# Recurrent attention with a squared-relu layer on one core: weight casts on GpSimd, separate q and k transpose banks, more dummies at the start, later planned load times

## The chip, the cores and the metric

The kernel runs on one core of a Trainium2 chip. Its engines are TensorE (PE in the profile, with PEld for its weight loads), VectorE (DVE), ScalarE (ACT) and GpSimd (POOL); SyncE (SP) issues every DMA. The metric is the device time of one execution in microseconds; the median of three runs before the change is 195.5 us (195.12 to 195.73). Each engine takes its own instructions in the order in which they were written, and waits for the others by semaphores.

## The reference, cut to what matters

Four batches of eight heads, 768 tokens, head size 48. A state of 48 x 48 per head decays by `alpha` and takes up k times v; q reads it. All heads of a token together are a row of `x` (3072 tokens x 384), and the second part multiplies `x` with `w_in` (384 x 2048), squares the relu, and multiplies with `w_out` (2048 x 384).

```python
for t in range(S):
    state = alpha[:, :, t, :, None] * state + np.einsum('bhd,bhe->bhde', k[:, :, t], v[:, :, t])
    y[:, :, t] = np.einsum('bhd,bhde->bhe', q[:, :, t], state)
x = np.ascontiguousarray(y.transpose(0, 2, 1, 3)).reshape(B * S, H * D)
h = x @ w_in
r = np.maximum(h, 0.0)
out = (r * r) @ w_out
```

## The kernel before

**Tiles.** The 3072 tokens are 24 chunks of 128. Inside a chunk the recurrence becomes matmuls: the logarithm of alpha (`e_ln`, L563 on ACT) is summed along the tokens by a triangular matmul (`e_p0`, the only one with `utri_b`), A and Ainv are the exponentials of the sum with both signs (L582, L586 on ACT), `qA_s` and `kI_s` are q times A and k times Ainv (L601, L604 on DVE), PE turns both (`e_p1q`, `e_p1k`, four transposes each), DVE copies the turned tiles out of PSUM (L558), scores go to `sc`, DVE masks them into `sm` (L642), and PE multiplies with v (`vb`, cast by POOL at L568) and with the state. The result is copied to bf16 (`xn`, ACT L556), turned and stored in `xT_big`. The first four chunks go as two **sets** of two chunks each (`add_set`, L340), with instructions at L352 (ln), L380 (A and Ainv), L384 (products, one of them on POOL), L415 and L417 (copies of turned tiles on ACT and DVE), L454 (masks) and L485 (state).

**The layer behind it.** M1 is `xT_big` times `w_in_b` into a PSUM bank (three banks take turns), then relu on ACT (L746), then the square on DVE (L754, one tile `r` as both of its inputs) into `gT`. M2 is `w_out_b` times `gT`, sixteen matmuls of 128x384 for a chunk, in four quarters; the result leaves by L786 on ACT and a DMA (L794, L796). Chunks are grouped: the first group has four chunks, then one, one, and two at a time. M1 and M2 of ready chunks are the work that fills PE between the steps of the recurrence.

**Weights.** `load_w` (L277) loads w_in in five pieces (two of 128x768 float32, three of 128x1536) and w_out in four of 128x1536 into a four-buffer stage, and casts each to bf16. A piece's load waits for the cast of the piece four before it. The engine of a cast is picked by the planner: eight on DVE (L300), one on ACT (L302).

**Loads of the chunks.** `add_load` (L317) issues four DMAs a chunk (at, qt, kt, vt: alpha, q, k, v; 192 KB each, L324), `add_load2` (L330) four of 384 KB a set (L337). There are buffers for six chunks.

**The planner.** Nothing above is written in its final order. Each step is an `Op` with an engine, a planned duration, the ops it needs and a priority, and `Plan.run` places all ops on planned time lines; the instructions are then written out by planned start. A load has a planned duration and `lat`, the planned time from its end on the queue to its landing: 2.0 us for sets and chunks below 4, 2.4 us from chunk 4 on. An ACT op that needs a load (`e_ln`) is placed at the planned landing, with priority over the relus. What stands behind it on ACT waits with it. The gate (`LEAD`, L835) keeps `e_p0` of a chunk from being planned too far ahead of M1 and M2.

**Banks and dummies.** `GLA_BANKS` are two PSUM banks for all small steps of the recurrence; a `Slots` object says when a bank is free again (the op in `gives`). In `add_turn` (L420) a set's chunk j takes one bank for its turned q and its turned k together, so q of both chunks is turned first, then k of both into the same two banks. Until the first M2, planned gaps of PE are filled with dummy matmuls of a zero tile `warm` (L850 to L863): seven of 128x512 at the start, then one of 128x256 for each 0.11 us of a planned gap.

Of the kernel before, what the change touches and what calls it, by code (L numbers as in the profile page):

```python
# [9 lines left out]
BF16 = mybir.dt.bfloat16  # L10
# [9 lines left out]
class Slots:  # L20
# [5 lines left out]
    def free_at(self):  # L26
        n = len(self.release) - self.bufs
        if n < 0:
            return 0.0
        op = self.release[n]  # L30
        return None if op.done is None else op.done


LAT = {"PE": 0.13, "ACT": 0.14, "DVE": 0.13, "POOL": 0.25}
# [20 lines left out]
def after(op, x=0.0):  # L55
    return (op, x)
# [83 lines left out]
def kernel(  # L140
# [10 lines left out]
    nc = tc.nc  # L151
    B, H, S, D = q.shape
    HD = H * D
    P = 128
    DP = 64
    NP = H // 2
# [32 lines left out]
    ident_bf = consts.tile([P, P], BF16)  # L189
# [4 lines left out]
        out=utri_f, in_=utri_f, compare_op=ALU.is_ge, fill=0.0,  # L194
# [46 lines left out]
    def pin(ins):  # L241
        tc.keep_in_program_order(ins)
# [4 lines left out]
    def tr(*a):  # L247
        pin(nc.tensor.transpose(*a))  # L248

    plan = Plan()  # L250
# [4 lines left out]
    GLA_BANKS = sl_bank[0:2]  # L255
# [13 lines left out]
    def add(eng, dur, emit, *deps, **kw):  # L269
        return plan.add(Op(eng, dur, emit, deps, **kw))  # L270
# [6 lines left out]
    def load_w(which):  # L277
        j = len(w_ready[which])
        lo, hi = W_CUT[which][j:j + 2]
        n = hi - lo  # L280
        box = {}

        def halves(t):
            return t.rearrange("p j (a f) -> p a j f", a=2) if which == "i" else t
        if which == "i":
            src, dst = w_in_r[:, :, lo * P:hi * P], w_in_b[:, :, lo * P:hi * P]
            shape = [P, KT, n * P]
        else:
            src, dst = w_out_r[:, lo:hi, :], w_out_b[:, lo:hi, :]
            shape = [P, n, d_model]  # L290

        def e_issue():
            box["w"] = stage.tile(shape, FP32, name=f"w{which}{n}", tag="stage")
            pin(nc.sync.dma_start(out=box["w"], in_=src))

        def e_cast():
            if op.eng == "POOL":
                pin(nc.gpsimd.tensor_copy(dst, box["w"]))
            elif op.eng == "DVE":
                pin(nc.vector.tensor_copy(halves(dst), halves(box["w"])))  # L300
            else:
                pin(nc.scalar.copy(dst, box["w"]))  # L302
        prev = w_cast[-SB] if len(w_cast) >= SB else None
        ld = add("DMA", WLD * n / 4 + 0.03, e_issue, prev, lat=2.0)
        op = add({"POOL": 0.1 + 0.75 * n, "DVE": 0.1 + 0.2 * n, "ACT": 0.1 + 0.32 * n}, 0, e_cast, ld, prio=-3.0)
        w_cast.append(op)
        w_ready[which].append(op)

# [8 lines left out]
    def add_load(s, nm):  # L317
        d = C[s]
        b, c = divmod(s, NCH)

        def ld():
            i = s % LB
            d[nm] = ld_s[nm][:, i * HD:(i + 1) * HD].rearrange("p (h d) -> p h d", h=H)
            pin(nc.sync.dma_start(out=d[nm], in_=SRC[nm][b, c]))  # L324
        prev = C[s - LB]["use_" + nm] if s >= LB else None
        d["ld_" + nm] = add("DMA", LD if s < 4 else LD1, ld, prev, lat=2.0 if s < 4 else 2.4, at=0.6)

    E = [dict() for _ in range(NSET)]

    def add_load2(u, nm):  # L330
        d = E[u]

        def ld():
            t = ld_s[nm][:, 2 * u * HD:(2 * u + 2) * HD]
            d[nm] = t.rearrange("p (h j d) -> p h j d", h=H, j=2)
            b, c = divmod(2 * u, NCH)
            pin(nc.sync.dma_start(out=t.rearrange("p (h e) -> p h e", h=H), in_=srcs2[nm][b, c // 2]))  # L337
        d["ld_" + nm] = add("DMA", LD2, ld, lat=2.0, at=0.6)

    def add_set(u):  # L340
        d = E[u]
# [15 lines left out]
            pin(nc.gpsimd.tensor_copy(d["vb"], d["vt"].rearrange("p h j d -> p j h d")))  # L357
        vb = add("POOL", 1.1, e_vb, d["ld_vt"], prio=-5.0)

        pm, A, Ai, exA, exI, mq, mk, cps = {}, {}, {}, {}, {}, {}, {}, {}  # L360

        def add_sum(j):
            def e_p0():
# [40 lines left out]
        def e_cp(op, j, lo):  # L404
            if "qT" not in d:
                d["qT"] = work.tile([P, NP, 2, 2, HP], BF16, name="qT2", bufs=2)
                d["kT"] = work.tile([P, 2, NP, P], BF16, name="kT2", bufs=2)
            if lo:
                cast2(op, d["kT"][:, j], d["pT"][j][:, NP:, :])
            else:  # L410
                cast2(op, d["qT"][:, :, :, j, :], d["pT"][j][:, 0:NP, :].rearrange("q p (c i) -> q p c i", c=2))

        def cast2(op, out_t, in_t):
            if op.eng == "ACT":
                pin(nc.scalar.copy(out_t, in_t))  # L415
            else:
                pin(nc.vector.tensor_copy(out_t, in_t))  # L417
        d["pT"] = {}

        def add_turn(j):  # L420
            def e_p1q():
                d["pT"][j] = psum(p1q, [P, 2 * NP, P], BF16)
                for p in range(NP):
                    tr(d["pT"][j][:, p, :], qA[:, j, 2 * p:2 * p + 2, :], ident_bf)

            def e_p1k():
                for p in range(NP):
# [283 lines left out]
    gT = {}  # L711
# [11 lines left out]
    def add_moe1(g, f0, before, lo=0, hi=None, per=1):  # L723
# [26 lines left out]
        def e_sq():  # L750
            if g not in gT:
                gT[g] = big.tile([P, FT, P * max(GN[g % NGT::NGT])], BF16, name=f"gT{g % NGT}", tag=f"gT{g % NGT}")
            r = box["r"][:, 0:w].rearrange("p (a n) -> p a n", a=per)
            pin(nc.vector.tensor_mul(gT[g][:, f0:f0 + per, lo * P:lo * P + n], r, r))  # L754
# [139 lines left out]
```

## Time and profile before

| | us |
|---|---|
| median of three runs | 195.5 (195.12 to 195.73) |
| the profiled execution | 196.74 |
| its span, first to last instruction | 195.0 |
| PE busy in the span | 184.0 (94%) |
| DVE, ACT, POOL busy | 131.7, 121.7, 15.8 |
| mean granted TensorE clock | 0.988 |

The profiled execution took 196.74 us, of which the instructions span 195.0. A row of the timeline is: start in us from the span's start, duration in us, engine and line, operation, output <- inputs, shape, count of merged instructions, and in brackets the idle time of that engine ahead of it with what ended it. A row of the windows is a stretch, its length, busy us of the engines with their instruction counts, the granted clock of TensorE, the busy share of the DMA engines and what they moved. A row of the waits is: who waited for whom, us in all, how often, the longest.

### The profile page before, as it was taken

How to read it: one execution, taken by the hardware profiler on the slowest of the kernel's cores; microseconds unless marked ns; L12 is line 12 of the kernel's file. 1: busy time of each engine (PE TensorE's matmuls, PEld its weight loads, DVE VectorE, ACT ScalarE, POOL GpSimd, SP SyncE). 2: the span in 40 equal slices, each digit the busy share in tenths (PEclk: the TensorE clock that was granted, in tenths of full speed). 3: DMA queues.
4: the chain of work that ended last, by engine and by line, in shares of the span. 5: the costliest groups of instructions: out<-in, count | busy, mean ns of one | idle time of the engine just before them, and what ended most of it. 6: DMA issues, size and time to landing. Idle time of an engine off the chain costs nothing.

```text
span 195.0 us, 5155 instructions
## 1 busy us (share of the span) xinstructions
PE 184.0 (94%) x2051; PEld 137.2 (70%) x2051; DVE 131.7 (68%) x288; ACT 121.7 (62%) x283; POOL 15.8 (8%) x35
## 2 busy tenths in 40 slices
PE   6888999999999969999999999999999999999991
PEld 2656788667887646867867867867868768768660
DVE  5479999957987835876767858858757857735100
ACT  3557689446977564946956956956955746628210
POOL 3104001011101111111110110110010000000000
PEclk9999999999999978999999999999999999999998
DMA  6999999999899899999999999470110110111121
GB/s 151 261 264 369 379 195 318 262 201 166 186 196 205 150 198 207 187 203 205 194 216 178 212 162 195 91 179 4 40 44 0 42 45 0 44 40 40 44 81 42
DMA packets 99176, 30.22 MB, mean 155 GB/s; under 512 B 92112, under 2 KB 98000, under 8 KB 99152
## 3 DMA queue, kind: packets, MB, share of 16 engines
q1 hardware_dynamic: 99152, 29.89, 72.3%
q8 instruction: 16, 0.26, 0.6%
q14 instruction: 8, 0.07, 0.1%
HBM read 25.17 MB, written 4.72 MB: 153 GB/s over the span
## 4 chain that ended last, share of the span: by engine, by line
PE 82%; DMA 6%; ACT 3%; DVE 3%; SPq 1%; issue 1%; POOL 0%; ACTq 0%; POOLq 0%; DVEq 0%
PE bank L245 70%; PE bank L248 7%; DMA at_s<-in_alpha_dram 4%; PE sc L245 3%; DMA vt_s<-in_v_dram 2%; PE st L245 2%; ACT r L746 1%; SPq L324 1%; DVE kI_s L384 1%; SPq L794 0%; DVE qA_s L384 0%; ACT L_s L352 0%; DVE sm L454 0%; DVE kT L417 0%; ACT qT L415 0%
## 5 line engine op out<-in xcount | busy, mean ns | idle before, releaser
L245 PE MATMUL bank<-xT_big,w_in_b 128*128 128x256 bf16 (+1 forms) x624 | 77.5, 264 | 2.2 <-ACT r L746 2.1
L245 PE MATMUL bank<-w_out_b,gT 128*128 128x384 bf16 x384 | 72.6, 330 | 0.0
L746 ACT ACTIVATE r<-bank 128x512 bf16<-128x512 f32 x96 | 56.5, 603 | 19.8 <-PE bank L245 17.4
L245 PEld LDWEIGHTS <-w_in_b 128*128 128x128 bf16 x624 | 53.1, 98 | 9.2 <-issue 2.5
L754 DVE TENSOR_TENSOR gT<-r 128x512 bf16<-128x512 bf16 x96 | 38.2, 420 | 16.8 <-ACT r L746 16.7
L245 PEld LDWEIGHTS <-gT 128*128 128x128 bf16 x384 | 35.6, 98 | 19.7 <-issue 1.0
L642 DVE TENSOR_TENSOR sm<-sc,utri_b 128x512 bf16<-128x512 f32 x40 | 25.6, 682 | 2.7 <-PE sc L245 2.7
L786 ACT COPY ob<-bank 128x384 f32<-128x384 f32 x24 | 11.5, 480 | 25.0 <-PE bank L245 25.0
L601 DVE TENSOR_TENSOR qA_s<-qt_s,A 128x384 bf16<-128x384 f32 x20 | 11.8, 588 | 13.2 <-ACT A L582 11.7
L568 POOL CAST vb<-vt_s 128x384 bf16<-128x384 f32 x20 | 11.1, 553 | 116.6 <-PE bank L245 54.0
L558 DVE COPY qkT<-bank 128x1024 bf16<-128x1024 bf16 x20 | 13.8, 691 | 6.6 <-PE bank L248 6.4
L563 ACT ACTIVATE L_s<-at_s 128x384 bf16<-128x384 f32 x20 | 10.4, 521 | 7.8 <-DMA at_s<-in_alpha_dram 7.6
L245 PEld LDWEIGHTS <-qkT 64*128 64x128 bf16 (+1 forms) x228 | 9.2, 95 | 5.8 <-issue 2.3
L604 DVE TENSOR_TENSOR kI_s<-kt_s,Ainv 128x384 bf16<-128x384 f32 x20 | 11.4, 568 | 1.0 <-DMA kt_s<-in_k_dram 1.0
L582 ACT ACTIVATE A<-bank 128x384 bf16<-128x384 f32 x20 | 10.0, 500 | 3.0 <-PE bank L245 3.0
L245 PEld LDWEIGHTS <-sm 128*128 128x128 bf16 (+1 forms) x224 | 8.8, 96 | 2.2 <-issue 0.8
L556 ACT CAST xn<-bank 128x384 bf16<-128x384 f32 x20 | 9.7, 483 | 0.6 <-PE bank L245 0.6
L586 ACT ACTIVATE Ainv<-bank 128x384 bf16<-128x384 f32 x20 | 10.1, 503 | 0.0
L248 PE MATMUL bank<-ident_bf,kI_s 128*128 128x128 bf16 x96 | 9.1, 219 | 0.9 <-DVE kI_s L604 0.5
L245 PE MATMUL bank<-vb,sm 128*128 128x48 bf16 (+1 forms) x224 | 9.8, 184 | 0.1
L248 PE MATMUL bank<-ident_bf,qA_s 128*128 128x128 bf16 x96 | 9.4, 224 | 0.0
L667 ACT CAST sb<-st 128x384 bf16<-128x384 f32 x16 | 7.6, 475 | 2.9 <-DVE st L662 2.8
(75 smaller groups left out, 161.8 us busy)
## 6 DMA issues: line engine op xcount, KB each, us to landing
at_s<-in_alpha_dram SPq DMA_DIRECT2D x20, 192.0 KB, 4.4
qt_s<-in_q_dram SPq DMA_DIRECT2D x20, 192.0 KB, 4.3
kt_s<-in_k_dram SPq DMA_DIRECT2D x20, 192.0 KB, 4.5
vt_s<-in_v_dram SPq DMA_DIRECT2D x20, 192.0 KB, 4.3
out_dram<-ob SPq DMA_DIRECT2D x20, 192.0 KB, 1.9
wo<-in_moe_w_out_dram SPq DMA_DIRECT2D x4, 768.0 KB, 7.8
wi<-in_moe_w_in_dram SPq DMA_DIRECT2D x3, 768.0 KB, 8.0
at_s<-in_alpha_dram SPq DMA_DIRECT2D x2, 384.0 KB, 4.9
```

The source lines that it names most:

```text
L245: pin(nc.tensor.matmul(*a, **kw))
L248: pin(nc.tensor.transpose(*a))
L558: pin(nc.vector.tensor_copy(out_t, in_t))
L563: pin(nc.scalar.activation(L[:, :, 0:D], d["at"], AF.Ln))
L568: pin(nc.gpsimd.tensor_copy(d["vb"], d["vt"]))
L586: pin(nc.scalar.activation(d["Ai"], d["pm"][:, 0:HD].rearrange("p (h d) -> p h d", h=H), AF.Exp, scale=-1.0))
L601: pin(nc.vector.tensor_mul(qA[:, :, 0:D], d["qt"], d["A"]))
L604: pin(nc.vector.tensor_mul(kI[:, :, 0:D], d["kt"], d["Ai"]))
L642: pin(nc.vector.tensor_mul(d["sm"][:, hh], d["sc"][:, hh], utri_b.to_broadcast([P, NP, P])))
L746: pin(nc.scalar.activation(box["r"][:, 0:w], box["ph"][:, 0:w], AF.Relu))
L754: pin(nc.vector.tensor_mul(gT[g][:, f0:f0 + per, lo * P:lo * P + n], r, r))
L786: pin(nc.scalar.copy(box["ob"], box["po"]))
```

## The change

- The casts of all nine weight pieces go to POOL, and only there; their planned duration is 0.1 + 0.5 us per 128-column block.
- `add_turn` no longer takes one bank per chunk for q and k; it takes one bank for q of both chunks and another for k of both chunks. All eight q transposes stand ahead of the two q copies, all eight k transposes ahead of the two k copies. A bank's release may now be a list of ops.
- Nine opening dummies of 128x512 where there were seven; below 9 us of planned time, one dummy for 0.16 us of planned gap where it was 0.11.
- `lat`: sets 2.0 to 2.5 us, chunks 4 and 5 stay at 2.4, later chunks 2.4 to 4.0 us.

```diff
@@ Slots.free_at
-        op = self.release[n]
-        return None if op.done is None else op.done
+        ops = self.release[n]
+        ops = ops if isinstance(ops, list) else [ops]
+        return None if any(op.done is None for op in ops) else max(op.done for op in ops)
@@ load_w
         def e_cast():
-            if op.eng == "POOL":
-                pin(nc.gpsimd.tensor_copy(dst, box["w"]))
-            elif op.eng == "DVE":
-                pin(nc.vector.tensor_copy(halves(dst), halves(box["w"])))
-            else:
-                pin(nc.scalar.copy(dst, box["w"]))
+            pin(nc.gpsimd.tensor_copy(dst, box["w"]))
...
-        op = add({"POOL": 0.1 + 0.75 * n, "DVE": 0.1 + 0.2 * n, "ACT": 0.1 + 0.32 * n}, 0, e_cast, ld, prio=-3.0)
+        op = add("POOL", 0.1 + 0.5 * n, e_cast, ld, prio=-3.0)
@@ add_load, add_load2
-        d["ld_" + nm] = add("DMA", LD if s < 4 else LD1, ld, prev, lat=2.0 if s < 4 else 2.4, at=0.6)
+        d["ld_" + nm] = add("DMA", LD if s < 4 else LD1, ld, prev, lat=2.4 if s < 6 else 4.0, at=0.6)
-        d["ld_" + nm] = add("DMA", LD2, ld, lat=2.0, at=0.6)
+        d["ld_" + nm] = add("DMA", LD2, ld, lat=2.5, at=0.6)
@@ add_set
-        def add_turn(j):
-            def e_p1q():
-                d["pT"][j] = psum(p1q, [P, 2 * NP, P], BF16)
-                for p in range(NP):
-                    tr(d["pT"][j][:, p, :], qA[:, j, 2 * p:2 * p + 2, :], ident_bf)
-
-            def e_p1k():
-                for p in range(NP):
-                    tr(d["pT"][j][:, NP + p, :], kI[:, j, 2 * p:2 * p + 2, :], ident_bf)
-            p1q = plan.add(Op("PE", 0.22, e_p1q, [mq[j]], takes=GLA_BANKS, **g))
-            p1k = plan.add(Op("PE", 0.22, e_p1k, [mk[j], after(p1q)], lat=0.15, **g))
-            cq = add({"ACT": 0.49, "DVE": 0.34}, 0, lambda: e_cp(cq, j, 0), p1q, **g)
-            ck = add({"DVE": 0.34, "ACT": 0.49}, 0, lambda: e_cp(ck, j, NP), p1k, after(cq, -9.0), **g)
-            p1q.gives = ck
-            return cq, ck
-        for j in range(2):
-            cps[j] = add_turn(j)
+        def add_turn(src, lo, ready):
+            ops = []
+            for j in range(2):
+                def e_p1(j=j):
+                    if j == 0:
+                        d["pT"][lo] = psum(ops[0], [P, 2, NP, P], BF16)
+                    for p in range(NP):
+                        tr(d["pT"][lo][:, j, p, :], src[:, j, 2 * p:2 * p + 2, :], ident_bf)
+                ops.append(plan.add(Op("PE", 0.22, e_p1, [ready[j], after(ops[0]) if j else None],
+                                       takes=None if j else GLA_BANKS, lat=0.15, **g)))
+            out = []
+            for j in range(2):
+                def e(j=j):
+                    e_cp(out[j], j, lo)
+                out.append(add({"ACT": 0.49, "DVE": 0.34}, 0, e, ops[1], **g))
+            ops[0].gives = out
+            return out
+        cq = add_turn(qA, 0, mq)
+        ck = add_turn(kI, NP, mk)
+        cps = [(cq[j], ck[j]) for j in range(2)]
@@ dummies
-    for _ in range(7):
+    for _ in range(9):
...
-                n = max(0, int((op.start - pe_end - 0.2) / 0.11))
+                n = max(0, int((op.start - pe_end - 0.2) / (0.11 if op.start > 9.0 else 0.16)))
```

In the order that the two programs are written out, these places differ around what follows. Chunk 5's `e_p0` has 24 M2 matmuls ahead of it where it had 28; the rest of the PE work ahead of it is the same, dummies apart. On ACT, `e_ln` of chunk 10 has 26 relus ahead of it where it had 28, that of chunk 11 has 30 relus and nine `xn` copies where it had 29 and eight. Between `e_ln` of chunk 10 and that of chunk 11 there was one relu; there are four. The DMAs of the sets and weights stand in the same order on SP. Around chunk 8 the output DMAs of the first group stand between its loads in pairs; before, two pairs stood together ahead of its q and a third ahead of its k. There are 28 dummies of both sizes where there were 31.

More of the change, by code (lines that the diff above doesn't have):

```diff
@@ L281, in load_w @@
         box = {}
-        def halves(t):
-            return t.rearrange("p j (a f) -> p a j f", a=2) if which == "i" else t
         if which == "i":
@@ L358, in add_set @@
         vb = add("POOL", 1.1, e_vb, d["ld_vt"], prio=-5.0)
-        pm, A, Ai, exA, exI, mq, mk, cps = {}, {}, {}, {}, {}, {}, {}, {}
+        pm, A, Ai, exA, exI, mq, mk = {}, {}, {}, {}, {}, {}, {}
         def add_sum(j):
@@ L408, in e_cp @@
             if lo:
-                cast2(op, d["kT"][:, j], d["pT"][j][:, NP:, :])
+                cast2(op, d["kT"][:, j], d["pT"][lo][:, j])
             else:
-                cast2(op, d["qT"][:, :, :, j, :], d["pT"][j][:, 0:NP, :].rearrange("q p (c i) -> q p c i", c=2))
+                cast2(op, d["qT"][:, :, :, j, :], d["pT"][lo][:, j].rearrange("q p (c i) -> q p c i", c=2))
         def cast2(op, out_t, in_t):
@@ L418, in add_set @@
         d["pT"] = {}
-        def add_turn(j):
-            def e_p1q():
-                d["pT"][j] = psum(p1q, [P, 2 * NP, P], BF16)
-                for p in range(NP):
-                    tr(d["pT"][j][:, p, :], qA[:, j, 2 * p:2 * p + 2, :], ident_bf)
-            def e_p1k():
-                for p in range(NP):
-                    tr(d["pT"][j][:, NP + p, :], kI[:, j, 2 * p:2 * p + 2, :], ident_bf)
-            p1q = plan.add(Op("PE", 0.22, e_p1q, [mq[j]], takes=GLA_BANKS, **g))
-            p1k = plan.add(Op("PE", 0.22, e_p1k, [mk[j], after(p1q)], lat=0.15, **g))
-            cq = add({"ACT": 0.49, "DVE": 0.34}, 0, lambda: e_cp(cq, j, 0), p1q, **g)
-            ck = add({"DVE": 0.34, "ACT": 0.49}, 0, lambda: e_cp(ck, j, NP), p1k, after(cq, -9.0), **g)
-            p1q.gives = ck
-            return cq, ck
-        for j in range(2):
-            cps[j] = add_turn(j)
+        def add_turn(src, lo, ready):
+            first = None
+            ops = []
[17 more added lines that the diff above has]
+        cps = [(cq[j], ck[j]) for j in range(2)]
         sc, sm, smo = {}, {}, {}
@@ L753, in e_sq @@
             r = box["r"][:, 0:w].rearrange("p (a n) -> p a n", a=per)
-            pin(nc.vector.tensor_mul(gT[g][:, f0:f0 + per, lo * P:lo * P + n], r, r))
+            dst = gT[g][:, f0:f0 + per, lo * P:lo * P + n]
+            pin(nc.vector.tensor_mul(dst, r, r))
         fr = sq[(g - NGT, "free")] if g >= NGT else None
```

## Prediction

> **What bounds the kernel now.** First the page: its span, the engines' busy time and the slices.
>
> ```profile
> span 195.0 us, 5155 instructions
> PE 184.0 (94%) x2051; PEld 137.2 (70%) x2051; DVE 131.7 (68%) x288; ACT 121.7 (62%) x283; POOL 15.8 (8%) x35
> PEclk9999999999999978999999999999999999999998
> ```
>
> PE is busy for 184.0 of 195.0 us, so time can be won only where PE idles, works on dummies or runs below its clock. Slices 14 and 15 (68 to 78 us) have a granted clock of 0.7 and 0.8. Next, who made PE wait, and on what ACT's logarithm waited:
>
> ```profile
> PE bank L245 <- ACT r L746: 2.1, 1, 2.1
> PE bank L248 <- DVE kI_s L604: 0.5, 1, 0.5
> ACT L_s L563 <- DMA at_s<-in_alpha_dram: 7.6, 5, 2.3
> ```
>
> Behind 20 us PE waits twice, for 0.5 and 2.1 us. The timeline there, with the two logarithms before it:
>
> ```profile
> 57.61 0.40 PE L248 MATMUL bank<-ident_bf,kI_s 128*128 128x128 bf16 x4 [0.48 <-DVE kI_s L604]
> 59.17 0.52 ACT L563 ACTIVATE L_s<-at_s 128x384 bf16<-128x384 f32 x1 [1.79 <-DMA at_s<-in_alpha_dram]
> 65.51 0.52 ACT L563 ACTIVATE L_s<-at_s 128x384 bf16<-128x384 f32 x1 [0.50 <-DMA at_s<-in_alpha_dram]
> 67.46 0.50 PE L245 MATMUL bank<-xT_big,w_in_b 128*128 128x256 bf16 x3
> 68.99 0.52 ACT L563 ACTIVATE L_s<-at_s 128x384 bf16<-128x384 f32 x1 [2.34 <-DMA at_s<-in_alpha_dram]
> 69.42 0.58 ACT L746 ACTIVATE r<-bank 128x512 bf16<-128x512 f32 x1
> 70.05 0.81 PE L245 MATMUL bank<-xT_big,w_in_b 128*128 128x256 bf16 x6 [2.09 <-ACT r L746]
> ```
>
> These are the logarithms of chunks 9, 10 and 11. ACT came to chunk 11's at 68.99 - 2.34 = 66.65 and stood until its load had landed; the relu behind it ran at 69.42, and PE, which needed the bank of that relu, stood for 2.09 us. The waits at chunks 9 and 10 (1.79, 0.50) cost PE nothing. After the stall the clock falls:
>
> ```profile
> 70.00:71.00 1.00, 0.95 (x11) 0.85 (x11) 0.52 (x2) 0.91 (x4) 0.00 (x0) 0.99 1.29 192
> 71.00:74.00 3.00, 3.00 (x22) 1.61 (x20) 1.19 (x3) 2.27 (x7) 0.51 (x1) 0.50 1.35 190
> 74.00:75.00 1.00, 1.00 (x8) 0.57 (x7) 0.59 (x2) 0.66 (x2) 0.00 (x0) 0.80 1.39 188
> ```
>
> Half clock for 3.4 us loses 0.01 + 3 x 0.50 + 0.20 = 1.71 us. Stalls and clock together are 0.48 + 2.09 + 1.71 = 4.28 us, the most that later `e_ln` positions can win. [...]
>
> **The change part by part: the load times.** `lat` from 2.4 to 4.0 us moves `e_ln` of chunks 6 and up, and all behind it, later in the order of ACT and PE. It changes no DMA; the DMA engines are saturated (busy share 1.29 and more in the rows above), so I let each load land when it landed before. Chunk 8's k loads sooner, past one pair of outputs fewer, and its turn stands later: the 0.48 is gone. Chunk 11's `e_ln` has one relu and one `xn` more ahead of it. That is at least the PE work of one relu, six matmuls from 64.76 to 65.41,
>
> ```profile
> 64.76 0.82 PE L245 MATMUL bank<-xT_big,w_in_b 128*128 128x256 bf16 x6
> 65.41 0.39 PE L248 MATMUL bank<-ident_bf,kI_s 128*128 128x128 bf16 x4
> 51.56 0.52 ACT L556 CAST xn<-bank 128x384 bf16<-128x384 f32 x1
> ```
>
> so 0.65 us, and at most ACT's time for both, 0.58 + 0.52 = 1.10; I take 1.0. But chunk 10's `e_ln` moves forward, by two relus: 2 x 0.65 = 1.3 less what takes their place (one `xn`, one `ob` copy, near 0.5 each on ACT): between 0.3 and 1.3, I take 1.0. There the wait goes. ACT came to it at 65.51 - 0.50 = 65.01; now at 65.01 - 0.48 - 1.0 + 0.2 (below) = 63.7, and waits 1.7 us, with relus and the `xn` for a turn on PE behind it. What PE pays lies between nothing (as with 1.79 at chunk 9) and 1.7; the one wait of such a length with relus behind it gave 2.09 of 2.34, so I take 1.2. Chunk 11 is then reached at 66.65 - 0.48 + 1.0 + 0.2 + 1.2 = 68.6 against a landing of 68.97: 0.4 us, which costs PE nothing. Half clock after 1.2 us of standing costs 0 (as after the 0.48) or 1.71 (as after the 2.09); 1.2 lies about midway, and I take 0, since no row shows a fall after less than 2.09.
>
> **The opening.** These rows carry it:
>
> ```profile
> 8.98 0.89 PE L248 MATMUL bank<-ident_bf,qA_s 128*128 128x128 bf16 x8
> 9.65 0.59 ACT L415 COPY qT<-bank 128x512 bf16<-128x512 bf16 x1 [1.06 <-PE bank L248]
> 10.29 0.61 PE L248 MATMUL bank<-ident_bf,kI_s 128*128 128x128 bf16 x8 [0.42 <-ACT qT L415]
> 11.26 0.42 PE L245 MATMUL sc<-qT,kT 64*64 64x128 bf16 x16
> 6.85 2.34 PE L245 MATMUL bank<-warm 128*128 128x256 bf16 x10
> 6.95 1.22 DVE L384 TENSOR_TENSOR qA_s<-qt_s,A 128x384 bf16<-128x384 f32 x2 [2.92 <-ACT A L380]
> 8.09 1.02 DVE L384 TENSOR_TENSOR kI_s<-kt_s,Ainv 128x384 bf16<-128x384 f32 x2
> 1.25 3.17 PE L245 MATMUL bank<-warm 128*128 128x512 bf16 x7 [1.25 <-DVE half L204]
> 5.41 0.48 PE L245 MATMUL bank<-L_s,incl 128*128 128x384 bf16 x1 [0.98 <-ACT L_s L352]
> ```
>
> The k transposes wait for the copy of q out of the same bank (10.29), though `kI_s` is ready at 9.11. With banks of their own they go at 9.2 and end near 9.8; the q copies run beside them, the first k copy (0.41 us on DVE) ends near 10.3, and the scores start at 10.3 instead of 11.26. Of ten dummies three go, 3 x 0.21 = 0.6 us of the wait of q's turn (ready at 8.17, turned at 8.98), inside the same chain. Two more opening dummies of 0.43 us spacing fill the 0.98 us of idle before 5.41, and cost nothing: the last starts near 4.6. So the opening wins about 1.0 us; the bounds are 0 and 1.1.
>
> It does not last. The next row of chunk 5:
>
> ```profile
> 39.04 0.52 ACT L563 ACTIVATE L_s<-at_s 128x384 bf16<-128x384 f32 x1 [1.66 <-DMA at_s<-in_alpha_dram]
> 40.12 0.33 PE L245 MATMUL bank<-L_s,utri_b 128*128 128x384 bf16 x1
> 40.38 2.11 PE L245 MATMUL bank<-w_out_b,gT 128*128 128x384 bf16 x12
> ```
>
> Chunk 5 keeps 2.4 us, its load lands at 39.0 behind three weight loads, and PE's first matmul of it needs the logarithm, done at 39.56. Now it has four M2 matmuls fewer ahead: 4 x 2.11/12 = 0.7 us. PE comes to it at 40.12 - 0.7 - 1.0 = 38.4 and stands until 39.6; the old program had come as far in its work by 40.12 - 0.7 = 39.4. The opening's gain ends as a loss of 0.2 us (bounds: -1.1, if the load lands sooner too, to +0.2).
>
> **The casts.** DVE and ACT lose what POOL takes over (the last row is the windows' view of the squares at L754 alone):
>
> ```profile
> 17.75 0.55 DVE L300 CAST w_in_b<-wi 128x768 bf16<-128x768 f32 x1
> L300 DVE CAST w_out_b<-wo 128x1536 bf16<-128x1536 f32 x4 | 3.8, 954 | 0.4 <-DMA wo<-in_moe_w_out_dram 0.3
> 9.13 0.83 POOL L357 CAST vb<-vt_s 128x768 bf16<-128x768 f32 x1 [6.02 <-DMA vt_s<-in_v_dram]
> 41.97 0.51 POOL L568 CAST vb<-vt_s 128x384 bf16<-128x384 f32 x1 [10.57 <-DMA vt_s<-in_v_dram]
> 14.94 0.91 POOL L384 TENSOR_TENSOR kI_s<-kt_s,Ainv 128x384 bf16<-128x384 f32 x1 [4.97 <-ACT Ainv L380]
> 15.40 0.86 DVE L384 TENSOR_TENSOR qA_s<-qt_s,A 128x384 bf16<-128x384 f32 x1
> 20.00:30.00 10.00, 9.94 (x149) 8.05 (x148) 9.99 (x21) 7.89 (x15) 0.00 (x0) 1.00 1.01 267
> 30.00:40.00 10.00, 10.00 (x103) 7.43 (x102) 9.48 (x19) 6.30 (x15) 0.65 (x1) 1.00 1.03 297
> 20.00:40.00 20.00, 5.90 (x16) 1.00 1.02 282
> ```
>
> DVE is relieved of 2 x 0.55 + 6 x 0.95 = 6.8 us. POOL takes 0.83 us for 768 elements and 0.51 for 384, so near 1.47 for 1536: 2 x 0.83 + 7 x 1.47 = 12.0 us in all. Where a cast ends later on POOL than it did on DVE, M1 is late ahead of 39 us, and the wait at chunk 5 swallows the first microsecond of that; what is late next is the squares. And a cast on POOL holds up DVE: `qA_s` met POOL's product (14.94 to 15.85), and ended 0.41 us after it, 0.86 us long instead of 0.56. [...] DVE's loss lies between 0 and 12.0 us; half a cast at each of nine, 6.0, is what a meeting at a random moment gives. Against 6.8 of relief I take nothing. [...]
>
> **The sum.** On the profiled execution, 196.74 us (195.0 of span and 1.74 around it): -4.28 + 1.2 + 0.2 = -2.88, so 193.9. The median of the runs is 1.24 us below that execution, so on it **192.6 us**.
>
> **The rivals.** *No wait takes the old one's place*: the loads land some 1 to 2 us sooner, the opening's gain is kept, 195.5 - 4.28 - 1.1 = 190.1. For it: the 1.79 us at chunk 9 cost PE nothing; against it: the DMA engines are full. *The wait at chunk 10 brings its own half clock*: 192.6 + 1.7 = 194.3. For it: the fall after 2.09 us; against: none after 0.48. *POOL's casts bind DVE*: the hold is the full 12.0 us, 5.2 more than the relief, of which DVE has 10.00 - 9.99 + 10.00 - 9.48 = 0.53 us spare between 20 and 40 us; M2's first quarters then wait for squares, 192.6 + 4.7 = 197.3, slower. It decides from a hold of 6.8 + 0.5 + 2.9 = 10.2 us on. For it: DVE is full there; against: a product or square would have to stand at the start of every cast, and DVE had only 16 squares and a few products to do between 20 and 40 us. *The change moves the stall but not its length*, with its half clock: 195.5.
>
> **How the numbers follow.** Forecast 0.43, no wait 0.12, second half clock 0.11, POOL binds 0.24, stall only moved 0.10. Differences under 0.3% (0.6 us) can't be told from none. Faster are the first three, 0.66; same 0.10; slower 0.24. The range goes from 190.4 (most of the first rival) to 197.2 (just short of the third's price); the forecast's own is 191 to 194.5.
>
> **What would show it.** No 2.09 us stall and no half clock near 70 us; a PE wait near 39 us before chunk 5's `utri_b` matmul; ACT waiting some 1.7 us at chunk 10's logarithm; scores of the first set near 10.3 us; DVE products of 0.8 us and more beside POOL casts of about 1.5. Wrong would be: squares a microsecond late with PE idle between 20 and 45 us, or a half clock anywhere behind 20 us.

## The result, and the profile after

The changed kernel took 193.15 us (median of 4 executions, 192.82 to 193.62), the kernel before beside it 195.31 (194.91 to 195.73): a ratio of 0.989, with a 95% interval of 0.986 to 0.992. That is 2.2 us faster. The profiled execution took 192.82 us, 3.9 less than the one of before. In the experiments the kernel before took longer than here, 197.2 to 197.5 us beside the changed kernels, and the mean TensorE clock of 30 of its 56 executions there is low (below); ratios are therefore taken within one group of runs only. Eight of those 30, of 197.6 to 199.9 us, count as slow and are left out of the ratios.

First the page of the changed kernel: span, engines, slices of the clock.

```profile
span 191.1 us, 5139 instructions
PE 181.2 (95%) x2048; PEld 134.9 (71%) x2048; DVE 129.2 (68%) x280; ACT 121.6 (64%) x282; POOL 27.2 (14%) x44
PEclk9999999999999999999999999999999999999998
```

Then the two waits of PE that lie behind 20 us, from the view of the waits:

```profile
PE bank L249 <- ACT xn L554: 1.1, 1, 1.1
PE bank L246 <- ACT L_s L561: 0.7, 1, 0.7
```

The 2.1 us behind the relu is gone, and no slice ahead of the end has a clock below 0.9. Two waits stand behind 20 us instead, 0.7 and 1.1 us. The timeline shows the first scores, the places of the two waits, at chunks 5 and 10, and chunk 11's logarithm without one:

```profile
10.02 0.42 PE L246 MATMUL sc<-qT,kT 64*64 64x128 bf16 x16 [0.39 <-DVE kT L411]
39.15 0.52 ACT L561 ACTIVATE L_s<-at_s 128x384 bf16<-128x384 f32 x1 [3.06 <-DMA at_s<-in_alpha_dram]
39.72 0.32 PE L246 MATMUL bank<-L_s,utri_b 128*128 128x384 bf16 x1 [0.73 <-ACT L_s L561]
65.47 0.52 ACT L561 ACTIVATE L_s<-at_s 128x384 bf16<-128x384 f32 x1 [1.59 <-DMA at_s<-in_alpha_dram]
66.41 0.34 PE L249 MATMUL bank<-ident_bf,xn 128*128 128x128 bf16 x3 [1.15 <-ACT xn L554]
69.09 0.52 ACT L561 ACTIVATE L_s<-at_s 128x384 bf16<-128x384 f32 x1
```

PE's last stretch, in the timeline of before and then of the changed kernel:

```profile
180.14 10.56 PE L245 MATMUL bank<-w_out_b,gT 128*128 128x384 bf16 x64
```

```profile
177.08 10.56 PE L246 MATMUL bank<-w_out_b,gT 128*128 128x384 bf16 x64
```

These 64 matmuls of M2 are the same in both, and start 3.06 us sooner. The other 0.84 us of the span lies behind PE: 195.0 - 190.70 = 4.30 us there before, 191.1 - 187.64 = 3.46 after.

### The profile page after: what moved, and what is told of

It reads as the page before. It is cut to its first block, busy times and chain, and to the rows that moved or that the text cites. A ratio compares the mean times of both kernels' runs of the same rounds, so it can differ in the third digit from the quotient of the medians.

```text
span 191.1 us, 5139 instructions
## 1 busy us (share of the span) xinstructions
PE 181.2 (95%) x2048; PEld 134.9 (71%) x2048; DVE 129.2 (68%) x280; ACT 121.6 (64%) x282; POOL 27.2 (14%) x44
## 4 chain that ended last, share of the span: by engine, by line
PE 70%; DMA 15%; SPq 7%; DVE 2%; ACT 2%; POOL 1%; issue 1%; ACTq 0%
PE bank L246 61%; DMA at_s<-in_alpha_dram 7%; PE bank L249 6%; SPq L331 5%; DMA wo<-in_moe_w_out_dram 4%; DMA wi<-in_moe_w_in_dram 4%; PE sc L246 3%; SPq L293 1%; PE st L246 1%; POOL w_out_b L296 1%; DVE sm L640 1%; ACT r L744 1%; SPq L793 1%; POOL w_in_b L296 0%; DVE qkT L556 0%
## 5 line engine op out<-in xcount | busy, mean ns | idle before, releaser
L246 PE MATMUL bank<-xT_big,w_in_b 128*128 128x256 bf16 (+1 forms) x624 | 75.9, 264 | 0.5
L246 PE MATMUL bank<-w_out_b,gT 128*128 128x384 bf16 x384 | 71.6, 326 | 0.0
L753 DVE TENSOR_TENSOR gT<-r 128x512 bf16<-128x512 bf16 x96 | 41.4, 447 | 12.8 <-ACT r L744 12.0
L246 PEld LDWEIGHTS <-gT 128*128 128x128 bf16 x384 | 34.9, 98 | 18.5
L566 POOL CAST vb<-vt_s 128x384 bf16<-128x384 f32 x20 | 10.6, 530 | 93.4 <-DMA vt_s<-in_v_dram 48.3
L556 DVE COPY xT_big<-bank 128x384 bf16<-128x384 bf16 x20 | 7.1, 354 | 13.1 <-PE bank L249 13.1
L660 DVE TENSOR_TENSOR st<-st,ae_s 128x384 f32<-128x384 f32 x16 | 8.9, 558 | 0.6 <-PE st L246 0.6
```

Source lines behind the costliest of these rows:

```text
L246: pin(nc.tensor.matmul(*a, **kw))
L566: pin(nc.gpsimd.tensor_copy(d["vb"], d["vt"]))
L753: pin(nc.vector.tensor_mul(dst, r, r))
```

## The experiments

Each kernel ran beside the kernel before in one group: the first four, the next four and the last four, each group on one chip. "PE waits" is the sum of the waits of 0.2 us and more behind 20 us that PE's timeline shows in that kernel's profile, one execution.

| run | median us | ratio to before, 95% | PE waits us |
|---|---|---|---|
| before again | 196.75 | 1.000, 0.996 to 1.004 | 3.8 |
| load times alone | 193.96 | 0.984, 0.979 to 0.989 | 1.5 |
| all but the load times | 196.50 | 0.997, 0.993 to 1.001 | 5.0 |
| all but the casts | 194.64 | 0.989, 0.983 to 0.994 | 3.5 |
| changed kernel again | 193.70 | 0.986, 0.980 to 0.992 | 1.7 |
| load times and casts | 193.43 | 0.984, 0.978 to 0.990 | 2.9 |
| changed, 4.0 us for chunk 5 | 193.63 | 0.986, 0.980 to 0.992 | 2.8 |
| changed, 5.5 us for chunk 10 | 193.83 | 0.986, 0.980 to 0.992 | 1.5 |
| changed, outputs late | 191.48 | 0.975, 0.969 to 0.981 | 1.3 |
| the same, 4.0 us for chunk 5 | 190.85 | 0.973, 0.966 to 0.979 | 0 |
| all but the dummies | 193.97 | 0.986, 0.981 to 0.991 | 2.3 |
| casts done twice | 200.88 | 1.021, 1.015 to 1.026 | 6.2 |

**Before again.** No edit.

> The kernel before, unchanged, to see what its executions have in common. Theory (load waits set the loss): every execution has the 2.09 us stall at chunk 11 and the half clock behind it, so the granted clock is 0.985 to 0.990 in each, the new profile shows both, and the median is 195.3. Rival (the fall of the clock is an accident of the one profiled execution, which lay 1.24 us above its median): most executions have a mean clock of 0.995 or more, those with 0.988 are about 1.7 us longer, and a new profile can lack the half clock.

The rival held. The granted clock over all 56 executions of before in these groups has two kinds: 25 with a mean of 0.994 and more, median 195.9 us, and 30 with 0.990 or less, median 197.9 (one lies between). Half clock as in the prediction's rows, 1.71 us of 195, takes 0.009 off a mean; where it fell in executions without a profile no trace shows. The new profile has a mean of 0.998: its page shows no fall in the slices,

```profile
PEclk9999999999999999999999999999999999999999
```

and its timeline the same stall at chunk 11:

```profile
70.69 0.52 ACT L563 ACTIVATE L_s<-at_s 128x384 bf16<-128x384 f32 x1 [2.48 <-DMA at_s<-in_alpha_dram]
71.75 0.82 PE L245 MATMUL bank<-xT_big,w_in_b 128*128 128x256 bf16 x6 [2.10 <-ACT r L746]
```

So the stall at chunk 11 belongs to the program, and the half clock behind it to some executions. Here the loads landed later (chunk 11's logarithm at 70.69 instead of 68.99), and other stalls brought the span to 194.9 all the same.

**Load times alone**, on the kernel before:

```diff
-        d["ld_" + nm] = add("DMA", LD if s < 4 else LD1, ld, prev, lat=2.0 if s < 4 else 2.4, at=0.6)
+        d["ld_" + nm] = add("DMA", LD if s < 4 else LD1, ld, prev, lat=2.4 if s < 6 else 4.0, at=0.6)
...
-        d["ld_" + nm] = add("DMA", LD2, ld, lat=2.0, at=0.6)
+        d["ld_" + nm] = add("DMA", LD2, ld, lat=2.5, at=0.6)
```

> Before plus the load times alone (2.4, and 4.0 from chunk 6 on; sets 2.5). In this order chunk 11's logarithm has two relus more ahead of it than before (31 instead of 29, as many xn), chunk 10's as many as before. Theory (load waits): ACT comes to chunk 11 about 1.3 us later, its wait falls from 2.34 to 1.0 or less and PE's stall from 2.09 to 0 to 0.8; no half clock; the 0.48 at chunk 8 is gone: 195.3 - 0.48 - 1.3 to 2.1 - 1.7 = 191.0 to 191.8, better than the changed kernel, since chunk 10 has no new stall. Rival 1 (the gain is the opening's): 195.0 to 195.5, with the stall in place. Rival 2 (the stall counts, the half clock is an accident): 192.7 to 193.5.

**All but the load times** is the changed kernel with these two edits turned back.

> The changed kernel with the old load times (2.0, 2.4 from chunk 4 on; sets 2.0). Chunk 11's logarithm has one relu more ahead than before (30), and so has chunk 10's (29). Theory (load waits): a stall of 1.4 to 2.0 us stays at chunk 11, the 0.48 at chunk 8 too: 195.3 - 0.2 to 0.7 = 194.6 to 195.1 if the half clock follows the stall, 193.0 to 193.4 if it doesn't. Rival (opening and casts bring the gain): 193.2, as the changed kernel, with the same waits as it has.

The two are complements, and the answer is in their ratios: 0.984 for the load times alone, 0.997 for all the rest. PE's waits with the load times alone (two rows of that view),

```profile
PE bank L245 <- ACT r L746: 1.0, 2, 0.8
PE bank L248 <- ACT xn L556: 0.6, 1, 0.6
```

the logarithms of chunks 10 and 11 in the same kernel's timeline,

```profile
65.83 0.52 ACT L563 ACTIVATE L_s<-at_s 128x384 bf16<-128x384 f32 x1 [1.20 <-DMA at_s<-in_alpha_dram]
69.68 0.52 ACT L563 ACTIVATE L_s<-at_s 128x384 bf16<-128x384 f32 x1 [1.15 <-DMA at_s<-in_alpha_dram]
```

and the timeline of all the rest, chunk 11's logarithm and two stalls of PE:

```profile
69.83 0.52 ACT L561 ACTIVATE L_s<-at_s 128x384 bf16<-128x384 f32 x1 [2.35 <-DMA at_s<-in_alpha_dram]
72.13 0.34 PE L249 MATMUL bank<-ident_bf,xn 128*128 128x128 bf16 x3 [1.69 <-ACT xn L554]
80.08 0.82 PE L246 MATMUL bank<-xT_big,w_in_b 128*128 128x256 bf16 x6 [1.61 <-ACT r L744]
```

The load lands near 69.7 in both. With 31 relus ahead of it (30 in all the rest, 29 before) ACT waits 1.15 us for it instead of 2.35, and PE 0.58 behind that instead of 1.69. At chunk 10 ACT waited 1.20, which was not expected, and PE 0.76 for it: in place of 191.0 to 191.8 stands 193.96, beside a before that took 197.3 on this chip. The gain, 3.1 us by the ratio, is no smaller than the whole change's. About 1 us of it is the clock: all six executions with the load times alone have a mean of 0.996 and more, and against the executions of before of that kind (195.9) the gain is 1.9 us. All the rest came to 196.50 with a low clock in three of twelve executions alone (0.989 to 0.991), where 193.0 to 193.4 was expected without the half clock: the 1.61 us at 80.08 were not foreseen.

**All but the casts:** the changed kernel with the casts on DVE and ACT as in the kernel before (the helper `halves` is left out here).

```diff
...
-            pin(nc.gpsimd.tensor_copy(dst, box["w"]))
+            if op.eng == "POOL":
+                pin(nc.gpsimd.tensor_copy(dst, box["w"]))
+            elif op.eng == "DVE":
+                pin(nc.vector.tensor_copy(halves(dst), halves(box["w"])))
+            else:
+                pin(nc.scalar.copy(dst, box["w"]))
...
-        op = add("POOL", 0.1 + 0.5 * n, e_cast, ld, prio=-3.0)
+        op = add({"POOL": 0.1 + 0.75 * n, "DVE": 0.1 + 0.2 * n, "ACT": 0.1 + 0.32 * n}, 0, e_cast, ld, prio=-3.0)
```

> The changed kernel with the casts of the weights on DVE and ACT again, by the old costs. The plan then puts 28 relus ahead of chunk 10's logarithm instead of 26, and 31 ahead of chunk 11's instead of 30. Theory (load waits; the casts cost and win nothing by themselves): the 1.15 us stall of PE at chunk 10 is gone and none comes in its place: 193.15 - 1.15 = 192.0. Rival 1 (DVE's 6.8 us of relief are worth something): 193.5 to 195. Rival 2 (POOL's casts held DVE up as well): below 191.5.

The stall at chunk 10 went, as the order said, but 1.06 came at chunk 9 and 1.27 at chunk 11: in this execution the loads landed up to 2.8 us later than in the first profile of the changed kernel. The ratio, 0.989, cannot be told from the changed kernel's 0.986; a worth of DVE's relief of some tenths of a microsecond is not excluded by this pair.

**The changed kernel again, and load times with casts.** The second is the kernel before with the two load-time edits and the change's `e_cast`.

> The changed kernel, unchanged, beside the three that follow and the kernel before. Executions of before came in two kinds: a mean clock of 0.995 and more with 195.4 to 196.7 us, and 0.986 to 0.989 with 197.1 to 198.4. Theory (the half clock needs the long stall, and comes behind it only in some executions): none of the changed kernel's executions shows a clock near 0.988 with a fall behind 20 us, and its ratio to before depends on how many of before's do: 0.984 to 0.992. Rival (the fall comes by chance, whatever the stalls): a good share of them have 0.986 to 0.989 too, and are about 1.8 us longer.

> Before plus the load times and the casts on POOL, without the turn banks and the new dummies. From chunk 5 on its order on PE and ACT is the changed kernel's. Theory (the opening's microsecond ends at chunk 5's load): first scores at 11.2 to 11.5 instead of 10.0, but chunk 5's first matmul where the changed kernel has it (within 0.4 us), with a wait of 0 to 0.2 before it in place of 0.73, and the whole time within 0.5 us of the changed kernel's. Rival (the opening's gain is kept): 0.8 to 1.2 us slower than the changed kernel.

Chunk 5's first matmul started at 39.84 in the one and 39.95 in the other, and the medians differ by 0.3 us: the opening's part of the change brings nothing that can be measured. Not as expected, the kernel with the old opening had its first scores at 9.84, and so PE stood 0.98 us at chunk 5; the last but one experiment takes that up. The pair thus has no late opening in its profiles. The load times alone have one, first scores at 11.27, and still come to chunk 5 at nearly the same time, without a wait:

```profile
40.06 0.33 PE L245 MATMUL bank<-L_s,utri_b 128*128 128x384 bf16 x1
```

Of the changed kernel's ten executions in the result and here two have a mean clock of 0.990 and 0.991, and none is below; of the 36 of the six kernels nearest to it (load times and casts, the two with more slack, the two with late outputs, all but the dummies) ten have 0.989 to 0.991. So a low clock is rarer than before, and not gone. The one profile among these, of all but the dummies (0.991), has the half clock from 18 to 21.5 us, ahead of chunk 5's wait.

**More slack at chunk 5, and at chunk 10.** The new values for both:

```diff
-        d["ld_" + nm] = add("DMA", LD if s < 4 else LD1, ld, prev, lat=2.4 if s < 6 else 4.0, at=0.6)
+        d["ld_" + nm] = add("DMA", LD if s < 4 else LD1, ld, prev, lat=2.4 if s < 5 else 4.0, at=0.6)
```

```diff
-        d["ld_" + nm] = add("DMA", LD if s < 4 else LD1, ld, prev, lat=2.4 if s < 6 else 4.0, at=0.6)
+        d["ld_" + nm] = add("DMA", LD if s < 4 else LD1, ld, prev, lat=2.4 if s < 6 else 5.5 if s == 10 else 4.0, at=0.6)
```

> The changed kernel with 4.0 us for chunk 5 too: twelve M2 matmuls (2.1 us) more ahead of chunk 5's first matmul. Theory (0.73 us are lost there): the wait is gone and the gain shows in the whole time, 0.3 to 0.9 us better than the changed kernel. Rival (the loads behind it set the pace as far as 75 us, so PE only waits later): the wait at chunk 10 grows from 1.15 by as much, and the time is the changed kernel's within 0.3 us.

> The changed kernel with 5.5 us for chunk 10 alone: one relu and one xn more (1.1 us of ACT) ahead of its logarithm. Theory (the order around that logarithm costs PE 1.15 us): ACT waits 0.5 us or less there instead of 1.6, PE's stall falls to 0 to 0.3, the time by 0.6 to 1.1 us. Rival (the loads set the pace): a stall of 0.5 us or more shows at chunk 11 or 12 instead, and the time is the same within 0.3 us.

Both times the time came out as the rival had it: 193.63 and 193.83 against 193.70. With chunk 5 later, ACT's and PE's rows at chunk 9 and PE's at chunk 10 are:

```profile
61.08 0.52 ACT L561 ACTIVATE L_s<-at_s 128x384 bf16<-128x384 f32 x1 [3.37 <-DMA at_s<-in_alpha_dram]
61.66 0.32 PE L246 MATMUL bank<-L_s,utri_b 128*128 128x384 bf16 x1 [1.29 <-ACT L_s L561]
66.95 0.34 PE L249 MATMUL bank<-ident_bf,xn 128*128 128x128 bf16 x3 [0.79 <-ACT xn L554]
```

The 0.73 us at chunk 5 are gone, and 1.29 stand at chunk 9, one chunk ahead of where the rival had them. The alpha of chunk 9 came later: with twelve M2 matmuls more ahead of chunk 5, eight output DMAs instead of six stood ahead of it in SP's queue, and it was issued at 57.70 instead of 54.97:

```profile
57.70 0.59 SPq L318 DMA_DIRECT2D at_s<-in_alpha_dram  x1
```

With chunk 10 later, ACT does not wait there at all and 0.25 us at chunk 11, but 2.28 at chunk 12, and PE stands behind a relu that follows it:

```profile
74.61 0.81 PE L246 MATMUL bank<-xT_big,w_in_b 128*128 128x256 bf16 x6 [0.64 <-ACT r L744]
```

Shifting one wait leaves the next; what is left to win must come from the landing itself.

**Outputs late.** The outputs of chunks 0 to 7 stay in two stages that the weights no longer need, and their DMAs are written out 30 us behind the planned time instead of 3.5; PE and ACT keep their order.

```diff
+    OUT_FIRST = 30.0
...
-            box["ob"] = opool.tile([P, d_model], FP32, name="ob")
+            s = GT[g] + tt
+            if s < 8:
+                if s % 4 == 0:
+                    state["ob4"] = stage.tile([P, 4, d_model], FP32, name="ob4", tag="stage")
+                box["ob"] = state["ob4"][:, s % 4, :]
+            else:
+                box["ob"] = opool.tile([P, d_model], FP32, name="ob")
...
-        add("OUT", 0.55, e_out, ev, at=0.0).late = OUT_LATE
+        add("OUT", 0.55, e_out, ev, at=0.0).late = OUT_LATE if GT[g] + tt >= 8 else OUT_FIRST
```

> The changed kernel with its first eight outputs kept in the two free weight stages, and their DMAs put behind chunk 10's to 13's loads in SP's queue; the order on PE and ACT is unchanged. Theory (what lands late behind 45 us makes the stalls at chunks 9 to 12, and the outputs ahead of the loads make it late): the logarithms of chunks 9 to 12 wait 0.5 us or less, PE's stalls behind 45 us (1.15 to 2.3 us in the changed kernel and its near kin) are gone, the 0.7 to 1.0 at chunk 5 stays: 0.9 to 1.9 us better than the changed kernel. Rival (PE's order, or the relus, make the stalls): stalls of 1 us and more stay, no gain.

The theory held: 191.48 us, while the changed kernel without its dummies took 193.97 in the same group. By the ratios, 0.975 against 0.986, that is 2.2 us, somewhat more than the 0.9 to 1.9 expected; PE's last stretch starts at 175.35 instead of 177.08. SP's queue in the changed kernel's timeline, the alpha loads of chunks 9 to 11 and the outputs between them and behind,

```profile
54.97 1.23 SPq L318 DMA_DIRECT2D at_s<-in_alpha_dram  x1
58.02 1.73 SPq L793 DMA_DIRECT2D out_dram<-ob  x2
60.42 0.68 SPq L318 DMA_DIRECT2D at_s<-in_alpha_dram  x1
64.90 0.93 SPq L318 DMA_DIRECT2D at_s<-in_alpha_dram  x1
67.60 0.68 SPq L795 DMA_DIRECT2D out_dram<-ob  x1
```

the same loads and the first outputs in this kernel's,

```profile
52.17 0.95 SPq L318 DMA_DIRECT2D at_s<-in_alpha_dram  x1
56.94 0.98 SPq L318 DMA_DIRECT2D at_s<-in_alpha_dram  x1
60.55 0.93 SPq L318 DMA_DIRECT2D at_s<-in_alpha_dram  x1
76.34 2.01 SPq L800 DMA_DIRECT2D out_dram<-ob  x2
```

and ACT at chunks 10 and 11, from the same timeline:

```profile
63.80 0.54 ACT L561 ACTIVATE L_s<-at_s 128x384 bf16<-128x384 f32 x1
67.81 0.52 ACT L561 ACTIVATE L_s<-at_s 128x384 bf16<-128x384 f32 x1
```

Chunk 10's alpha is issued at 56.94 instead of 60.42 and chunk 11's at 60.55 instead of 64.90; neither logarithm waits, and no PE wait is left behind 45 us. In the changed kernel a pair of outputs stands between these loads, and none does here until 76.34.

**Outputs late, and 4.0 us for chunk 5:** both edits above.

> The last one with 4.0 us for chunk 5 too. With chunk 5's 4.0 us alone, the stall only went from chunk 5 to chunk 9 and no time was won. Theory (both stalls are one lateness of the loads): with the outputs out of the way neither stall is left, PE waits less than 0.5 us in all behind 20 us, and the time is 0.3 to 0.9 us below the last run's, 1.5 to 2.5 below the changed kernel's. Rival: a wait comes back elsewhere between 40 and 80 us, and the time is the last run's.

Now the wait at chunk 5 goes for good: no wait of PE of 0.2 us or more behind 20 us, 190.85 us (5 of 6 executions from 190.51 to 191.16), ratio 0.973. This version beats both kernels.

**All but the dummies:**

```diff
-    for _ in range(9):
+    for _ in range(7):
...
-                n = max(0, int((op.start - pe_end - 0.2) / (0.11 if op.start > 9.0 else 0.16)))
+                n = max(0, int((op.start - pe_end - 0.2) / 0.11))
```

> The changed kernel with seven opening dummies and the old spacing of 0.11. In profiles so far TensorE came to its full rate near 5.5 us in all six with nine dummies, in one of four with seven, and near 9 us in the other three; the one with seven that was early had its first scores at 9.84 without the turn banks. Theory A (the dummies bring the opening forward, the turn banks nothing): first scores at 10.8 to 11.5 where the rate comes late. Theory B, the prediction's (the turn banks do): 10.3 or less even then. The whole time in both within 0.5 us of the changed kernel's, since chunk 5's load swallows a microsecond; rival: 0.8 to 1.2 us slower.

TensorE came to its full rate early here (the 128x384 matmul at 5.42 took 0.32 us; at 5.41 in before, 0.48), so neither condition arose; but the run stands beside "load times and casts", which was early too and differs by the turn banks alone. The copies and scores of the first set, without the turn banks and then with them:

```profile
8.23 0.59 ACT L410 COPY qT<-bank 128x512 bf16<-128x512 bf16 x1 [0.28 <-PE bank L248]
8.49 0.42 DVE L412 COPY qT<-bank 128x512 bf16<-128x512 bf16 x1
9.36 0.76 DVE L412 COPY kT<-bank 128x512 bf16<-128x512 bf16 x2 [0.45 <-PE bank L248]
9.84 0.42 PE L245 MATMUL sc<-qT,kT 64*64 64x128 bf16 x16
```

```profile
8.50 0.59 ACT L409 COPY qT<-bank 128x512 bf16<-128x512 bf16 x1 [0.51 <-PE bank L249]
9.12 0.42 DVE L411 COPY qT<-bank 128x512 bf16<-128x512 bf16 x1 [0.47 <-ACT qT L409]
9.46 0.42 DVE L411 COPY kT<-bank 128x512 bf16<-128x512 bf16 x1
9.93 0.42 PE L246 MATMUL sc<-qT,kT 64*64 64x128 bf16 x16 [0.39 <-DVE kT L411]
```

Without them the two q copies, out of two banks, run beside each other. With them both q copies read one bank, and DVE's starts only when ACT's has ended (9.12). What the k transposes win the copies lose. The whole time, 0.986 of before, is the changed kernel's, as expected.

**Casts done twice:**

```diff
             pin(nc.gpsimd.tensor_copy(dst, box["w"]))
+            pin(nc.gpsimd.tensor_copy(dst, box["w"]))
```

> The changed kernel with each cast of the weights done twice on POOL, one behind the other: 12 us more of POOL between 16 and 42 us, and the weights ready one cast later. Theory (a cast holds only the DVE instruction that happens to stand, and DVE has room since the casts left it): squares up to 6 us slower in sum, PE stalls of 0 to 2 us between 20 and 40 us that chunk 5's wait takes in: 0 to 1 us slower than the changed kernel. Rival (POOL's casts bind DVE): 4 to 5 us slower, with PE idle for squares between 25 and 45 us.

The theory fell: 200.88 us, some 7 above the changed kernel (0.986 of before) and more than the rival's 4 to 5. The windows' view of the squares alone, of the changed kernel and then of this one:

```profile
20.00:40.00 20.00, 7.79 (x16) 1.00 0.99 280
```

```profile
20.00:45.00 25.00, 16.39 (x16) 0.91 1.00 260
```

POOL, DVE and PE in this one's timeline:

```profile
28.21 1.54 POOL L297 CAST w_in_b<-wi 128x1536 bf16<-128x1536 f32 x1
29.70 1.65 POOL L296 CAST w_out_b<-wo 128x1536 bf16<-128x1536 f32 x1
28.88 5.33 DVE L754 TENSOR_TENSOR gT<-r 128x512 bf16<-128x512 bf16 x5
40.27 0.40 PE L246 MATMUL sc<-qkT 64*128 64x128 bf16 x8 [1.93 <-DVE qkT L557]
```

Sixteen squares took 5.90 us before, 7.79 in the changed kernel and 16.39 here. While POOL casts without a pause, most squares last until a cast has ended: of the five in 5.33 us four end 0.3 us behind the end of a POOL cast, and the fifth, with POOL idle, takes 0.41. What is queued behind the squares on DVE is then late for PE (1.93 us at 40.27). Not all of the 7 us is this hold. PE waits 1.23 us for pieces of w_in, which are ready one cast later, and this profile has half clock from 17.85 to 21.26 and from 41.74 to 45.15, 1.7 us each; the first stands in "all but the dummies" too, the second follows the 1.93. No run separates these parts.

## Why the prediction was right, point by point

Direction and size came out (192.6 forecast, 193.15 measured), the size in part by luck, because two errors offset each other: without the half clock, which the medians hardly held, the same sum gives 195.5 - 2.88 + 1.71 = 194.3, and 0.84 of gain came from a term that it lacked.

**The load times: right.** The 0.48 and the 2.09 us are gone. At chunk 10 ACT waited 1.59 (forecast 1.7) and PE 1.15 (forecast 1.2), with no half clock behind it; chunk 11's logarithm found its load there (forecast: 0.4 us of waiting, nothing for PE). The load times alone give 0.984, all the rest 0.997. One count is off: the traces have as many `xn` copies of single chunks ahead of chunk 11's logarithm as before (five), and one fewer, not one more, ahead of chunk 10's; the nine against eight in the text ahead of the prediction are nine against seven on ACT, of which two belong to a set and ran near 25 us. ACT still came to chunk 10 at 65.47 - 1.59 = 63.88, where 63.7 was forecast. What the prediction took as fixed, "each load landed when it landed before", held in the result's profile (chunk 10's logarithm at 65.47 and 65.51) and not in the others: chunk 11's came between 68.3 and 71.2 us in the profiles of the first eight runs, whose orders differ, and with it PE's waits.

**The half clock: mis-sized.** The step said that stalls and clock together, 4.28 us, are there to win, and carried the result from the profiled execution to the median by a shift of 1.24. But the 1.71 us of half clock were in that execution, while by their mean clock 25 of 56 executions of before have none; the median of 195.5, close to the 195.9 of those, hardly held any. On the medians this term should have been near zero. The second rival's price, another half clock, was for the same reason a matter of chance and not of 1.2 us against 2.09.

**A term that was missing: what follows PE.** Behind PE's last matmul the span was 4.30 us before (4.26 in the second profile) and 3.46 after (3.47 in its second); the sum had it unchanged. By profile: -4.28 + 1.15 at chunk 10 + 0.30 at chunk 5 = -2.83, against -3.06 measured to PE's end, and 0.84 more behind it. On the medians, -2.88 + 1.71 - 0.84 = -2.0 against the -2.2 measured. This tail was 3.8 in the load times alone, in all but them and in all but the casts, and 3.4 to 3.6 in the eight later profiles. What shortens it was not tried.

**The opening: right in its end, wrong in its cause.** The first scores came at 10.02 (forecast 10.3) and the gain was swallowed at chunk 5, as forecast: PE stood 0.73 us there until 39.72, and the old program had come as far by 40.12 - 0.70 = 39.42, so 0.3 was lost (forecast 0.2). The step that failed is "the q copies run beside them": it has both copies beside the k transposes at once. They run one behind the other out of the shared bank, and the turn banks move the scores by nothing (9.84 without, 9.93 with, both with an early full rate; with a late one no run has the new banks). What moved them was TensorE's full rate, at 5.5 us instead of 9.5 in the profile of before: the dummies of 128x256 ahead of q's turn took 0.93 us for seven, and 2.34 for ten before.

**The casts: nothing, as taken, but by other numbers.** The hold was booked at 6.0 us, half a cast at each. The squares grew by 7.79 - 5.90 = 1.9 us. POOL waits 0.3 to 2 us for each weight piece, and squares that come in these gaps meet no cast. Load times with and without the casts give 0.984 and 0.984: the relief of DVE shows no worth either; PE had hardly waited for it. The third rival was a real danger, only not in this schedule: with the casts doubled it happens, and the kernel loses 7 us, in which the half clock and the later weights are contained, against the 4.7 it was given. That squares last until the cast beside them has ended is what that run shows, with four of five squares ending 0.3 us behind a cast; in the prediction it was the author's inference from one product (0.86 us beside POOL's instead of 0.56).

**The rivals.** "No wait takes the old one's place" did not come by this change, but late outputs and chunk 5's slack bring it about: 190.85, near the 190.1 it was priced at, though on another chip.

## What to carry to other kernels

A wait for a load came here from what stood ahead of the load in its queue (chunk 10's alpha was issued at 60.42 us behind a pair of outputs, and at 56.94 without them) and from what stood ahead of the waiting instruction on its engine (chunk 11's logarithm waited 2.35 us behind 30 relus, and 1.15 behind 31). Moving the instruction handed the wait to another chunk (0.73 us at chunk 5 became 1.29 at chunk 9), while moving the outputs, for which nobody waits, behind the loads removed PE's waits behind 45 us (0.975 of before instead of 0.986). The casts given to the idle POOL, which hold up DVE's squares here (7.79 us for sixteen instead of 5.90), cost nothing that could be measured (0.984 with them and without) as long as POOL paused for 0.3 to 2 us ahead of each piece; with the casts doubled the sixteen took 16.39 us, and the kernel some 7 more, with later weights and half clock in it. And a profile is one execution: a term in it that belongs to the execution (here a fall of the clock) must not be subtracted from a median.

## What the runs showed of the hardware that was not expected

**The clock fell behind short stalls, and did not fall behind long ones.** Behind 2.09 us it fell in one profile of before, behind 2.10 us in the other it did not. In "all but the dummies" it fell behind 0.95 us, as that kernel's timeline of PE shows,

```profile
17.45 0.50 PE L246 MATMUL st<-vb,kI_s 64*128 64x96 bf16 x8 [0.95 <-ACT sb L488]
```

and its windows, with the granted clock as the third number from the end:

```profile
18.00:20.00 2.00, 2.00 (x17) 1.61 (x15) 1.32 (x3) 0.88 (x2) 0.83 (x1) 0.53 1.03 382
20.00:22.00 2.00, 2.00 (x30) 1.39 (x29) 1.04 (x2) 0.60 (x1) 1.43 (x1) 0.62 1.05 389
```

The same 0.95 us stand in the profiles of the changed kernel, without a fall.

For the long stalls the traces give more numbers. The falls behind 20 us last 3.41 us each (70.98 to 74.40 in before, 41.74 to 45.15 in "casts done twice"), and the recorded times of the changes lie whole multiples of 3.413 us apart: in before the fall comes 61.44 us, 18 of them, behind the rise to the full rate at 9.54, and in "casts done twice" the fall at 41.74 comes 7 of them behind the one at 17.85. The windows of PE alone, of before in the 3.41 us ahead of its fall, and of before again in two such stretches that share its stall (they are cut at 71.33, 18 of them behind the rise near 9.9 there):

```profile
67.57:70.98 3.41, 1.32 (x14) 1.00 1.22 206
```

```profile
67.92:71.33 3.41, 1.74 (x20) 1.00 1.04 192
71.33:74.74 3.41, 2.99 (x34) 1.00 1.21 196
```

The first leaves PE idle for 2.09 us and the clock falls at its end; the others leave 1.67 and 0.42, and it does not. In "casts done twice" the 3.41 us ahead of the fall at 41.74 hold PE's wait of 1.93. That the idle time within one such stretch is what counts would be a reading of these three stalls, and is not shown: the falls at 18 us, in "all but the dummies" and "casts done twice", come behind a wait of 0.95 us.

**The full rate at the start came at different times.** With seven opening dummies TensorE had it ahead of 5.4 us in two profiles (the 128x384 matmul at 5.37 and 5.42 takes 0.32 us), and reached it at 9.3 to 9.9 in three (the same matmul, at 5.41 to 5.62, takes 0.48, and the eight transposes of q, at 8.98 to 9.20, take 0.66 to 0.95 instead of 0.61); with nine it had it by 6.8 in all nine (seven dummies of 128x256, from 6.2 to 6.8 on, take 0.93 us). The time without a matmul from 4.42 on does not tell the two kinds with seven apart: 0.98 to 1.20 us in the late three, 0.95 and 1.00 in the early two. Nine dummies leave about 0.2 to 0.6 us there. Whether they secure the early rate is likely by these counts, and not settled.
